# Causal attention in halves of 64 keys, in a fused attention and tanh-shrink kernel on one Trainium2 core

## The chip, the cores and the metric

The kernel runs on one core of one Trainium2 chip. The metric is the device time of one execution in microseconds (us), and lower is better. Engine names are those of the profile: PE is TensorE (its weight loads are a row of their own, PEld), DVE is VectorE, ACT is ScalarE, POOL is GpSimd and SP is SyncE. A letter q behind a name (SPq) means that engine's instruction queue.

## The reference

The first stage is causal linear attention with a decay `lam` per head; the second multiplies its output by `w_in`, takes `h - tanh(h)`, and multiplies by `w_out`.

```python
# q, k, v: (B=4, H=8, S=768, D=64) float32; lam: (8,)
Dmask = np.where(rel >= 0, lam[:, None, None] ** rel[None, :, :], 0.0)      # rel = i - j in a block
for b in range(nb):                                                        # blocks of 64 in the reference
    intra = np.einsum('bhic,bhjc->bhij', qb, kb) * Dmask[None]
    intra = np.einsum('bhij,bhjd->bhid', intra, vb)
    inter = np.einsum('bhid,bhde->bhie', qb * lam_pow[None], kv_state)
    out[:, :, sl] = intra + inter
    kb_dec = kb * rev_pow[None]                                            # lam ** (block - 1 - pos)
    kv_state = lam_block * kv_state + np.einsum('bhsd,bhse->bhde', kb_dec, vb)
x = out.transpose(0, 2, 1, 3).reshape(B * S, H * D)                         # (3072, 512)
h = x @ w_in                                                               # w_in (512, 2048)
return (h - np.tanh(h)) @ w_out                                            # w_out (2048, 512)
```

## The kernel before, in words

The kernel uses blocks of `BLK` = 128 positions, which gives the same result as the reference's 64. There are six groups `g` of one block each; a group holds that block of all four batches `b`, so 512 tokens. The eight heads are four pairs `p` of two heads `j` (head 2p + j). While the matrix products of group g run, the attention of group g + 1 is done in between. `attention(g)` makes two lists of pieces, one for the half (b = 0, 1) and one for (2, 3), and the code around the products places them: `att_transpose` (q and k with the head dimension on partitions), `att_scores`, `att_out`, `att_state`.

The two products are not plain: each is done by a scheme with seven smaller products instead of eight (`up`, `down`), for some of them twice in a row (`down_twice`, `inner_steps`). Their matmuls are full tiles of 128x128 weights against 128 or 256 moving columns. They fill nearly all of TensorE's time. The pieces of `w_out` sums come from DRAM into a ring of seven buffers `wb`, loaded by POOL (lines 602 to 608).

In this kernel every fp32 matmul of the program is two instructions in the trace, each with its weight load; I call each of the two a pass. The attention has four kinds of passes, named here as "contracted rows x weight columns, moving columns":

- `att_scores`, line 352: 64x128, 128 columns. The two heads j of a pair stand on partition halves, so two passes run side by side. One batch has 16 passes. The result `sp` (keys on partitions, queries on columns) is multiplied by the decay mask into `ss` on VectorE (line 356), 512 columns for each j.
- `att_out`, line 400: `state` against `qd`, 64x64, 128 columns, in the four quarters of the array. 32 passes for a half of two batches.
- `att_out`, line 406: `v` against `ss`, 128x64, 128 columns, 32 passes for a half. With line 400 it accumulates in `op`, which ScalarE copies to `xt` (line 410).
- `att_state`, line 374: decayed `k` against `v`, 128x64, 64 columns, 32 passes for a half. The decay of k is line 361 on VectorE.

In groups 0 and 1 q and k are transposed by TensorE (line 336); from group 2 on they are loaded in 32x32 blocks (line 143) and transposed by VectorE (line 331). k and v in natural order are loaded by one DMA of 256 KB each from SP's queue (line 131). Instructions marked with `keep_in_program_order` (or `tied`) keep their written order; the others are placed by a scheduler, engine by engine. Banks of TensorE's result memory for the attention come from one tag, `att`, with four buffers. The blocks of `w_in` and `w_out` are loaded (lines 205 to 210) and rounded by ScalarE and VectorE (lines 289 to 296) during the first 130 us; this is `weights(n)`.

Of the kernel before, what the change touches and what calls it, by code (L numbers as in the profile page):

```python
# [9 lines left out]
F32 = mybir.dt.float32  # L10
# [6 lines left out]
AL = mybir.AluOpType  # L17

BLK = 128
GB = 2  # L20
# [4 lines left out]
def kernel(  # L25
# [32 lines left out]
    nc = tc.nc  # L58
    B, H, S, D = q.shape
    NTOK, DM = out.shape  # L60
    DFF = moe_w_in.shape[1]
    NP = H // 2
# [10 lines left out]
    const = ctx.enter_context(tc.tile_pool(name="const", bufs=1))  # L73
    wpool = ctx.enter_context(tc.tile_pool(name="wpool", bufs=1))
    io = ctx.enter_context(tc.tile_pool(name="io", bufs=4))
    work = ctx.enter_context(tc.tile_pool(name="work", bufs=2))
# [13 lines left out]
    ident = const.tile([128, 128], F32)  # L90
    make_identity(nc, ident)
    lam_all = const.tile([128, H], F32)
    nc.scalar.dma_start(out=lam_all, in_=bass.AP(tensor=lam.tensor, offset=lam.offset, ap=[[0, 128], [1, H]]))

    mask = const.tile([128, 2, NP, BLK], F32)
    for j in range(2):
        for p in range(NP):
            h = 2 * p + j
            nc.vector.tensor_tensor_scan(out=mask[:, j, p, :], data0=lam_all[:, h:h + 1].to_broadcast([128, BLK]),
                                         data1=ident, initial=0.0, op0=AL.mult, op1=AL.add)  # L100

    fwd = const.tile([128, NP, BLK], F32)

# [8 lines left out]
            m *= 2  # L112


    bwd = mask.rearrange("s j p i -> s p j i")[:, :, :, BLK - 1:BLK].to_broadcast([128, NP, 2, D])

    lam_blk = fwd[:, :, BLK - 1:BLK][:, None, :, :].to_broadcast([128, 2, NP, D])

    def tied(yes, op):
        return tc.keep_in_program_order(op) if yes else op  # L120


    raw, late = {}, {}
# [3 lines left out]
    def load_natural(g, b, names):  # L127
        for name, src, bufs in (("q", q, 2), ("k", k, 3), ("v", v, 4)):
            if name in names:
                x = (qpool if name == "q" else io).tile([128, H, D], F32, name=f"{name}_nat", tag=name, bufs=bufs)  # L130
                op = nc.sync.dma_start(out=x, in_=src[b, :, ts(g, BLK), :].rearrange("h s d -> s h d"))  # L131
                tc.keep_in_program_order(op)
                raw[g, b][name] = x

    def load_blocks(g, b, names):
# [162 lines left out]
    def bank(name, tag, bufs):  # L298
        return psum.tile([128, 512], F32, name=name, tag=tag, bufs=bufs)
# [18 lines left out]
    state = const.tile([128, B, NP, D], F32)  # L318


    tr, sc, kdec, xt = {}, {}, {}, {}

    def att_transpose(g, bs):
        for b in bs:
# [17 lines left out]
                nc.vector.tensor_tensor(qd, qt, fwd, op=AL.mult)  # L342
            tr[g, b] = (qt, kt, qd)

    def att_scores(g, bs):
        for b in bs:
            qt, kt, _ = tr[g, b]

            sp = [bank("sp", "att", 4).rearrange("s (p i) -> s p i", p=NP) for _ in range(2)]
            for p in range(NP):  # L350
                for j in range(2):
                    tied(g == 0, nc.tensor.matmul(out=sp[j][:, p, :], lhsT=kt[ts(j, 64), p, :],  # L352
                                                  rhs=qt[ts(j, 64), p, :], start=True, stop=True))
            ss = work.tile([128, 2, NP, BLK], F32, name="ss", tag="ss")
            for j in range(2):
                tied(g == 0, nc.vector.tensor_tensor(ss[:, j], sp[j], mask[:, j], op=AL.mult))  # L356
            sc[g, b] = ss

    def att_decay(g, b):
        kp = raw[g, b]["k"].rearrange("s (p j) d -> s p j d", j=2)  # L360
        tied(g != 1, nc.vector.tensor_tensor(kp, kp, bwd, op=AL.mult))

    def att_state(g, bs):
        if g == NG - 1:
# [19 lines left out]
    def att_out(g, bs):  # L384
        half = bs[0] // 2
        xt[g, half] = xpool.tile([128, KI, HB], F32, name=f"xt{half}", tag=f"xt{half}")

        ops = [bank("op", "att", 4).rearrange("d (p b s) -> d p b s", p=2, b=2) for _ in range(2)]

        def dst(n, p, j):  # L390
            return ops[p // 2][ts(j if p < 2 else 1 - j, 64), p % 2, n, :]


        if g > 0:
            for n, b in enumerate(bs):
                for p in (0, 1):
                    for j in range(2):
                        r = ts(j, 64)
                        for pp in (p, p + 2):
                            nc.tensor.matmul(out=dst(n, pp, j), lhsT=state[r, b, pp, :], rhs=tr[g, b][2][r, pp, :],  # L400
                                             start=n == 0 and p == 0, stop=False, skip_group_check=True)
        for n, b in enumerate(bs):
            ss, vn = sc.pop((g, b)), raw[g, b]["v"]
            for p in range(NP):
                for j in range(2):
                    tied(g == 0, nc.tensor.matmul(out=dst(n, p, j), lhsT=vn[:, 2 * p + j, :], rhs=ss[:, j, p, :],  # L406
                                                  start=g == 0 and n == 0 and p % 2 == 0,
                                                  stop=n == 1 and p % 2 == 1, skip_group_check=True))
        for x in range(2):
            tied(g == 0, nc.scalar.activation(  # L410
                xt[g, half][:, 2 * x:2 * x + 2, :].rearrange("d p (b s) -> d p b s", b=2), ops[x], AF.Copy))
# [9 lines left out]
        xt[g] = dict(B11=b11, B21=b21, B22=b22, T1=tt[:, 0], T2=tt[:, 1], T3=b12, T4=tt[:, 2])  # L421

    def attention(g):
        pieces = [[(fn, g, bs) for fn in (att_transpose, att_scores, att_out, att_state)] for bs in ((0, 1), (2, 3))]
        pieces[1].append((att_sums, g, None))
        return pieces

# [133 lines left out]
    def twice(g, n):  # L561
        return n in TWICE and not (g == NG - 1 and n == 3)
# [154 lines left out]
            store(g, 12, o)  # L717
        yield

    def every(steps):  # L720
        for _ in steps:
            pass

    def down_end(g):

# [81 lines left out]
    def run(pieces):  # L807
        for fn, *args in pieces:
            fn(*args)


    for b in (0, 1):
# [4 lines left out]
    half = up_plain(0, (11, 21))  # L817
# [26 lines left out]
    p0, p1 = attention(1)  # L844
    load(B + 2)
    turns = [(1, 11, 1, ()), (1, 21, 1, ()), (1, 12, 1, ()), (1, 22, 1, ()), (2, 11, 2, p0[0:1]), (2, 21, 2, p0[1:2]),
             (3, 11, 1, ()), (3, 21, 1, p0[2:4]), (2, 12, 1, ()), (2, 22, 1, p1[0:1]), (3, 12, 1, p1[1:2]),
             (3, 22, 1, ())]
    for u, c, n, more in turns:
        every(up_plain(u, (c,)))  # L850
        weights(ready["done"] + n)
        run(more)
        if c == 22:
            sums_first(u)
            if u == 1:
                load_weights(NU * KI)
                load(2 * B)
                powers()
            if u == 2:
                sums_in(0)  # L860
    sums_out(0)
    run(p1[2:4])
    sums_out(1)
    weights(NU * KI + 6)
    load_weights(ready["done"] + WAHEAD)
    run(p1[4:])
    sums_late(0)
    for kt in range(KH):
        down_first(kt, (1, 2, 5, 4, 7, 6, 3) if kt + 1 < KH else (1, 2, 6, 5, 7, 3, 4))
# [17 lines left out]
    for g in range(1, NG):  # L887
        last = g == NG - 1
        p0, p1 = attention(g + 1) if not last else ([], [])
# [14 lines left out]
                run(p0[u - 2:u - 1])  # L904
        if twice(g, 4):
            sums_twice(g, 4)
        every(down(g, 2))
        run(p0[2:])
        sums_twice(g, 5)
        every(down_twice(g, 4, "z") if twice(g, 4) else down(g, 4))  # L910
        run(p1[0:1])
        sums_once(g, 21, 21, 11)
        sums_twice(g, 6)
# [1 line left out]
        run(p1[1:2])  # L915
        if twice(g, 7):
            sums_twice(g, 7)
        every(down_twice(g, 6, "z"))
        if twice(g, 3):
            sums_twice(g, 3)  # L920
        run(p1[2:])
        every(down_twice(g, 7, "w") if twice(g, 7) else down(g, 7))
        if last:
            down_end(g)
# [45 lines left out]
```

## Time and profile before

| | |
|---|---|
| time, three runs | 667.26, 668.35, 668.37 us; median 668.35 us |
| profiled execution | span 665.0 us from the first to the last instruction; its own total time is not on the page |
| what lies around the span | 668.35 - 665.0 = 3.3 us, by the median of the runs |
| PE busy | 653.9 us, 98% of the span |
| DVE busy | 480.1 us, 72% |
| ACT, POOL busy | 32%, 29% |
| granted TensorE clock | 1.000 |
| DMA | mean 183 GB/s |

A row of a group of instructions reads: line, engine, operation, out<-in by the program's names, shapes, count, then total busy time, mean ns of one, and the idle time before them with what ended it. Passes overlap on TensorE, so the mean of one (some 270 ns) is a latency; what a pass costs is the step from one start to the next.

### The profile page before, as it was taken

How to read it: one execution, taken by the hardware profiler on the slowest of the kernel's cores; microseconds unless marked ns; L12 is line 12 of the kernel's file. 1: busy time of each engine (PE TensorE's matmuls, PEld its weight loads, DVE VectorE, ACT ScalarE, POOL GpSimd, SP SyncE). 2: the span in 40 equal slices, each digit the busy share in tenths (PEclk: the TensorE clock that was granted, in tenths of full speed). 3: DMA queues.
4: the chain of work that ended last, by engine and by line, in shares of the span. 5: the costliest groups of instructions: out<-in, count | busy, mean ns of one | idle time of the engine just before them, and what ended most of it. 6: DMA issues, size and time to landing. Idle time of an engine off the chain costs nothing.

```text
span 665.0 us, 13269 instructions
## 1 busy us (share of the span) xinstructions
PE 653.9 (98%) x4992; PEld 594.7 (89%) x4992; DVE 480.1 (72%) x869; ACT 214.7 (32%) x413; POOL 195.8 (29%) x340
## 2 busy tenths in 40 slices
PE   8999999999999999999999999999999999999998
PEld 7788888888888999888999988999988899988897
DVE  4568898997778983579885379987368877357753
ACT  4778923423321112341112342112243112233110
POOL 0001416783112444001435101254301264400250
PEclk9999999999999999999999999999999999999999
DMA  9999936997345979425889543698731687610491
GB/s 216 231 205 263 300 123 215 352 316 219 81 93 145 303 221 276 80 35 135 226 247 277 146 74 73 165 286 255 216 72 38 186 260 258 222 37 1 116 295 64
DMA packets 158958, 121.74 MB, mean 183 GB/s; under 512 B 133872, under 2 KB 135024, under 8 KB 158896
## 3 DMA queue, kind: packets, MB, share of 16 engines
q0 software_dynamic: 26400, 86.27, 40.4%
q1 hardware_dynamic: 132352, 34.64, 25.3%
q8 instruction: 39, 0.64, 0.4%
q14 instruction: 23, 0.19, 0.1%
q10 hardware_dynamic: 144, 0.00, 0.0%
HBM read 100.67 MB, written 20.19 MB: 182 GB/s over the span
## 4 chain that ended last, share of the span: by engine, by line
PE 66%; issue 14%; DMA 8%; SPq 4%; POOL 3%; DVE 3%; ACT 1%; POOLq 0%; DVEq 0%; ACTq 0%
PE y L458 13%; PE y L693 12%; PE zw L693 9%; PE z L458 8%; PE y L542 4%; PE w L640 4%; PE y L640 4%; PE sp L352 2%; PE z L542 2%; DMA raw<-in_moe_w_in_dram 2%; PE h L748 2%; DMA wb<-fine 2%; PE op L406 2%; SPq L131 2%; SPq L143 1%
## 5 line engine op out<-in xcount | busy, mean ns | idle before, releaser
L605 POOL DMA_DIRECT2D wb<-fine x168 | 90.5, 539 | 170.3 <-PE y L693 55.9
L466 ACT ACTIVATE th<-g 128x512 f32<-128x512 f32 x76 | 47.6, 630 | 99.5 <-DVE g L471 34.2
L696 ACT ACTIVATE q<-y 128x128 f32<-128x128 f32 x96 | 26.6, 277 | 149.6 <-PE y L693 148.6
L458 PE MATMUL y<-xt,w 128*128 128x256 f32 x320 | 73.5, 380 | 0.0
L458 PEld LDWEIGHTS y<-xt,w 128*128 128x128 f32 x320 | 59.9, 190 | 8.5 <-ACT g L546 0.9
L467 DVE TENSOR_TENSOR g<-g,th 128x512 f32<-128x512 f32 x76 | 52.1, 689 | 21.1 <-ACT th L466 21.0
L693 PE MATMUL y<-wb,g 128*128 128x128 f32 x456 | 60.6, 278 | 0.0
L748 PE MATMUL h<-xt,w 128*128 128x256 f32 x256 | 58.0, 383 | 2.0 <-DVE w L296 2.0
L748 PEld LDWEIGHTS h<-xt,w 128*128 128x128 f32 x256 | 47.7, 190 | 9.9 <-DVE w L296 2.7
L693 PEld LDWEIGHTS y<-wb,g 128*128 128x128 f32 x456 | 55.1, 192 | 1.3 <-issue 0.3
L608 POOL DMA_DIRECT2D wb<-factors x44 | 23.8, 541 | 96.0 <-PE y L640 64.6
L693 PE MATMUL zw<-wb,g 128*128 128x128 f32 x304 | 40.3, 275 | 0.1
L458 PE MATMUL z<-tt,ws 128*128 128x256 f32 x160 | 38.1, 381 | 0.0
L458 PE MATMUL y<-tt,ws 128*128 128x256 f32 x160 | 37.8, 379 | 0.0
L458 PE MATMUL z<-xt,ws 128*128 128x256 f32 x160 | 37.8, 379 | 0.0
L693 PEld LDWEIGHTS zw<-wb,g 128*128 128x128 f32 x304 | 37.0, 192 | 0.2 <-DVE g L698 0.2
L640 PE MATMUL w<-wb,g 128*128 128x256 f32 x160 | 35.8, 382 | 0.0
L640 PE MATMUL y<-wb,g 128*128 128x256 f32 x160 | 35.3, 379 | 0.0
L356 DVE TENSOR_TENSOR ss<-sp,mask 128x512 f32<-128x512 f32 x48 | 31.1, 684 | 5.8 <-PE sp L352 5.8
L640 PEld LDWEIGHTS y<-wb,g 128*128 128x128 f32 x160 | 30.4, 190 | 4.1
L458 PEld LDWEIGHTS z<-xt,ws 128*128 128x128 f32 x160 | 30.4, 190 | 4.1
L640 PEld LDWEIGHTS w<-wb,g 128*128 128x128 f32 x160 | 30.1, 190 | 4.4
(178 smaller groups left out, 1292.6 us busy)
## 6 DMA issues: line engine op xcount, KB each, us to landing
wb<-fine POOLq DMA_DIRECT2D x168, 256.0 KB, 4.2
wb<-factors POOLq DMA_DIRECT2D x44, 256.0 KB, 4.5
v_nat<-in_v_dram SPq DMA_DIRECT2D x24, 256.0 KB, 5.2
wb<-fine_in POOLq DMA_DIRECT2D x24, 256.0 KB, 4.3
k_nat<-in_k_dram SPq DMA_DIRECT2D x20, 256.0 KB, 5.0
raw<-in_moe_w_out_dram POOLq DMA_DIRECT2D x10, 512.0 KB, 4.9
raw<-in_moe_w_in_dram SPq DMA_DIRECT2D x8, 512.0 KB, 6.0
raw<-in_moe_w_in_dram SPq DMA_DIRECT2D x16, 256.0 KB, 5.6
```

The costliest lines, as they stand in the source:

```text
L131: op = nc.sync.dma_start(out=x, in_=src[b, :, ts(g, BLK), :].rearrange("h s d -> s h d"))
L356: tied(g == 0, nc.vector.tensor_tensor(ss[:, j], sp[j], mask[:, j], op=AL.mult))
L458: nc.tensor.matmul(out=t[:, m, :], lhsT=wt[:, kt, ts(m, 128)], rhs=x[:, kt, :], start=first and m == 0 and kt == 0, stop=kt == 1, skip_gro ...
L466: nc.scalar.activation(th, src, AF.Tanh)
L467: nc.vector.tensor_tensor(dst(c), src, th, op=AL.subtract)
L542: nc.tensor.matmul(out=dst[:, ts(u, 128)], lhsT=a, rhs=b, start=x in (1, 2, 5) and u == 0, stop=True, skip_group_check=True)
L605: nc.gpsimd.dma_start(out=t.rearrange("p m c -> p (m c)"), in_=fine[TWICE.index(n_), SUB.index(x_)].rearrange("p u c -> p (u c)"))
L608: nc.gpsimd.dma_start(out=t, in_=factors[XAT[FACT[n_][1]]][:, 2 * x_:2 * x_ + 2, :])
L640: nc.tensor.matmul(out=t[:, m, :], lhsT=a[:, u, kt, ts(m, 128)], rhs=wb[:, kt, :], start=first and u == 0 and m == 0 and kt == 0, stop=u = ...
L693: nc.tensor.matmul(out=dst, lhsT=a[:, u, :], rhs=wb[:, ts(u, 128)], start=x in (1, 2) and u == 0, stop=u == NU - 1, skip_group_check=True)
L696: nc.scalar.activation(keep, dst, AF.Copy)
L748: tied(u == 0, nc.tensor.matmul(out=hm[c][:, m, :], lhsT=w1[u][:, i, a, ts(m, 128)], rhs=xt[0, t][:, i, :], start=m == 0 and i == 0, stop= ...
```

## The change

Each block of 128 keys is split in two halves of 64 (`HF`). An early key can meet all 128 queries; a late key can only meet the 64 late queries. So the scores of a head become one product of 64 early keys with 128 queries and one of 64 late keys with 64 queries. The quarter "late keys, early queries" of the masked matrix, which is zero, is no longer computed.

For heads 4 to 7 the two key halves are exchanged on the partitions: k and v of these heads are loaded with late keys on partitions 0 to 63 and early keys on 64 to 127. Therefore early scores of heads 0 to 3 fall on the lower partition half and those of heads 4 to 7 on the upper one, and four consecutive passes use the four quarters of the array. In `sp` and `ss` a head pair has three column groups of 64 (`c`): 0 is early keys with early queries, 1 and 2 hold early and late keys with late queries, which together fill all 128 partitions.

`att_out`'s line 406 becomes two: late queries take all 128 keys (128x64, 64 columns), early queries take 64 keys (64x64, 64 columns). The mask is built for this layout; its multiplication is 384 columns for each j instead of 512. The decay of k becomes two instructions of 256 columns, because the mask columns that it uses differ between the head halves. k and v loads become three DMAs each. The matmuls with `state` move out of `att_out` into a new step `att_read`, which runs right behind the scores of the half's first batch; the scores of the second batch, `att_out` and `att_state` are placed later, inside the products around them.

```diff
+    HF = BLK // 2
+    mask = const.tile([128, 4, 3, HF], F32)
...
+    for n in range(4):
+        for dst, x in ((mask[:, n, 0:2].rearrange("s c i -> s (c i)"), 0), (cross[:, n], 1)):
+            w = dst.shape[-1]
+            nc.vector.tensor_tensor_scan(out=dst, data0=lam_x[:, x, n:n + 1].to_broadcast([128, w]), data1=inj[:, 0:w],
+                                         initial=0.0, op0=AL.mult, op1=AL.add)
+    for a, to, src in ((1, 2, mask[:, :, 1]), (1, 1, cross), (0, 2, cross)):
+        nc.vector.tensor_copy(mask[ts(a, HF), :, to], src[ts(a, HF)])
...
-                op = nc.sync.dma_start(out=x, in_=src[b, :, ts(g, BLK), :].rearrange("h s d -> s h d"))
-                tc.keep_in_program_order(op)
+                if name == "q":
+                    tc.keep_in_program_order(
+                        nc.sync.dma_start(out=x, in_=src[b, :, ts(g, BLK), :].rearrange("h s d -> s h d")))
+                else:
+                    for rows, hs, at_ in ((slice(0, BLK), 0, 0), (slice(0, HF), NP, HF), (slice(HF, BLK), NP, 0)):
+                        n = rows.stop - rows.start
+                        part = src[b, hs:hs + NP, g * BLK + at_:g * BLK + at_ + n, :]
+                        tc.keep_in_program_order(nc.sync.dma_start(out=x[rows, hs:hs + NP], in_=part.rearrange("h s d -> s h d")))
...
+    def att_read(g, bs):
+        ops = [bank("op", "att", 4).rearrange("d (p b s) -> d p b s", p=2, b=2) for _ in range(2)]
...
+                            tc.keep_in_program_order(nc.tensor.matmul(
+                                out=dst(n, pp, j), lhsT=state[r, b, pp, :], rhs=tr[g, b][2][r, pp, :],
+                                start=n == 0 and p == 0, stop=False, skip_group_check=True))
...
-            for p in range(NP):
-                for j in range(2):
-                    tied(g == 0, nc.tensor.matmul(out=sp[j][:, p, :], lhsT=kt[ts(j, 64), p, :],
-                                                  rhs=qt[ts(j, 64), p, :], start=True, stop=True))
+            for q in range(2):
+                for j in range(2):
+                    for p in (q, q + 2):
+                        tied(g == 0 or (b % 2 == 1 and (q, j, p) == (0, 0, 0)), nc.tensor.matmul(out=sp[j][half(p, False), q, 0:2 + p // 2:1 + p // 2, :],
+                                                      lhsT=keys(p, j, False), rhs=qt[ts(j, 64), p, :], start=True, stop=True))
+            for q in range(2):
+                for j in range(2):
+                    for p in (q, q + 2):
+                        tied(g == 0, nc.tensor.matmul(out=sp[j][half(p, True), q, 1 + p // 2, :], lhsT=keys(p, j, True),
+                                                      rhs=qt[ts(j, 64), p, HF:BLK], start=True, stop=True))
...
+    def att_scores_read(g, bs):
+        att_scores(g, bs[:1])
+        att_read(g, bs)
...
-        kp = raw[g, b]["k"].rearrange("s (p j) d -> s p j d", j=2)
-        tied(g != 1, nc.vector.tensor_tensor(kp, kp, bwd, op=AL.mult))
+        for e in range(2):
+            kp = raw[g, b]["k"][:, ts(e, NP)]
+            tied(g != 1, nc.vector.tensor_tensor(kp, kp, bwd[e], op=AL.mult))
...
+                    tied(whole, nc.tensor.matmul(out=dst(n, p, j)[:, HF:BLK], lhsT=vn[:, 2 * p + j, :],
+                                                  rhs=ss[:, j, p % 2, 1 + p // 2, :],
+                                                  start=g == 0 and n == 0 and p % 2 == 0,
+                                                  stop=True, skip_group_check=True))
...
-                    tied(g == 0, nc.tensor.matmul(out=dst(n, p, j), lhsT=vn[:, 2 * p + j, :], rhs=ss[:, j, p, :],
-                                                  start=g == 0 and n == 0 and p % 2 == 0,
-                                                  stop=n == 1 and p % 2 == 1, skip_group_check=True))
+            for q in range(2):
+                for p in (q, q + 2):
+                    for j in range(2):
+                        r = ts(p // 2, HF)
+                        tied(whole, nc.tensor.matmul(out=dst(n, p, j)[:, 0:HF], lhsT=vn[r, 2 * p + j, :],
+                                                      rhs=ss[r, j, q, 0, :], start=False, stop=True,
+                                                      skip_group_check=True))
...
-        pieces = [[(fn, g, bs) for fn in (att_transpose, att_scores, att_out, att_state)] for bs in ((0, 1), (2, 3))]
+        pieces = [[(att_transpose, g, bs), (att_scores_read, g, bs), (att_scores, g, bs[1:]), (att_out, g, bs),
+                   (att_state, g, bs)] for bs in ((0, 1), (2, 3))]
...
-        every(down(g, 2))
-        run(p0[2:])
+        product = down(g, 2)
+        steps(product, 2)
+        run(p0[2:3])
+        every(product)
         sums_twice(g, 5)
-        every(down_twice(g, 4, "z") if twice(g, 4) else down(g, 4))
+        product = down_twice(g, 4, "z") if twice(g, 4) else down(g, 4)
+        steps(product, 2)
+        run(p0[3:])
+        every(product)
...
-        every(down_twice(g, 6, "z"))
+        product = down_twice(g, 6, "z")
+        steps(product, 3)
+        run(p1[2:3])
+        every(product)
```

## The prediction

> **What bounds the kernel now.** I read the page's busy times first, then the chain that ended last in order of time, then TensorE's groups by shape, then TensorE's rows in a short window, and SP's queue at the start.
>
> ```profile
> span 665.0 us, 13269 instructions
> PE 653.9 (98%) x4992; PEld 594.7 (89%) x4992; DVE 480.1 (72%) x869; ACT 214.7 (32%) x413; POOL 195.8 (29%) x340
> ```
>
> TensorE is busy 98% of the span at a granted clock of 1.000; by windows it is busy 25.3 of the first 30 us, and from there to the end of the chain nearly all of every window (30.0 of 30 us from 80 to 110, 50.0 of 50 from 170 to 220). So a microsecond of TensorE work taken out is a microsecond of time, unless a wait takes its place. The time of the runs' median is 668.35 us, 3.3 us above the span; I take those 3.3 us as unchanged. The attention's share, from TensorE's groups by shape (the last two numbers ahead of the idle time are busy us and mean ns):
>
> ```profile
> L352 PE MATMUL sp<-qt,kt 64*128 64x128 f32 x384 | 25.2, 279 | 1.4 <-ACT kt L338 1.4
> L406 PE MATMUL op<-ss,v_nat 128*64 128x128 f32 x384 | 23.6, 275 | 0.0
> L374 PE MATMUL kv<-v_nat,k_nat 128*64 128x64 f32 x320 | 11.3, 223 | 0.0
> L400 PE MATMUL op<-qd,state 64*64 64x128 f32 x320 | 11.0, 275 | 0.0
> ```
>
> Only 71 of 665 us are attention, and the change touches the first two rows, 48.8 us. Next the timeline of TensorE, second half of one group; the first column is the start, and what a block costs is the distance to the next start:
>
> ```profile
> 229.76 2.06 PE L352 MATMUL sp<-qt,kt 64*128 64x128 f32 x32
> 231.75 1.16 PE L693 MATMUL y<-wb,g 128*128 128x128 f32 x8
> 232.74 1.06 PE L693 MATMUL zw<-wb,g 128*128 128x128 f32 x8
> ...
> 238.20 1.10 PE L400 MATMUL op<-qd,state 64*64 64x128 f32 x32
> 239.23 1.97 PE L406 MATMUL op<-ss,v_nat 128*64 128x128 f32 x32
> 241.03 1.10 PE L374 MATMUL kv<-v_nat,k_nat 128*64 128x64 f32 x32
> 242.06 0.71 PE L693 MATMUL y<-wb,g 128*128 128x128 f32 x4
> ```
>
> Blocks cost 1.99, 1.03, 1.80 and 1.03 us. Inside a block the starts step evenly; per pass, once running: line 352 56.0 ns (pairs 112 apart), line 400 27.3 ns (four starts within 20 ns, next four 109 ns after the first), line 406 54.5 ns, line 374 29.0 ns (pairs 58 apart), full tiles 112 ns for 128 columns. The rest is change of tile shape: the last pass before and the first pass after take 90 to 100 ns and 50 to 100 ns longer than their step. The two changes around line 352 cost 0.39 us in all, the three around the other block 0.51.
>
> **The change on TensorE, for one half of a group (two batches).** Before: 32 passes x 56.0 + 32 x 54.5 + 32 x 27.3 (state) + 32 x 29.0 (kv) + 0.90 for five changes of shape = 6.23 us. It repeats in ten halves (groups 1 to 5).
>
> After, by the order of instructions on TensorE:
> - First block: scores of batch one (16 early passes, 64x64 with 128 columns; 16 late, 64x64 with 64 columns) and 32 state passes, all one shape. Early passes have line 400's shape: 16 x 27.3 = 0.44; state 0.87; in and out 0.15 + 0.19.
> - Second block: scores of batch two, 0.44 early, 16 late; in and out 0.34.
> - Third block: 32 passes 128x64 with 64 columns for late queries, line 374's shape: 32 x 29.0 = 0.93; 32 passes 64x64 with 64 columns for early queries; kv 0.93; four changes, 0.14 to 0.19 each, 0.62.
>
> Sum: 2 x 0.44 + 0.87 + 0.93 + 0.93 + 1.29 = 4.90 us, and 64 passes of a shape that no row has: 64x64 with 64 columns, at x ns. The half gains 1.34 us - 64x. It breaks even at x = 21 ns.
>
> Bounds for x: from above line 400, the same quarters with twice the columns, 27.3 ns; from below line 374, whose 64 columns need 58 ns for a pair: if four quarters run in those 58 ns, x = 14.5. Line 400 shows four different quarters starting within 20 ns, so four fit into 58. A pass and its weight load are two instructions, so this needs one each 7.3 ns; in three places TensorE's queue, released from a semaphore wait, reaches the next semaphore 16 instructions later 143 ns after, at most 8.9 ns each, and it runs some 34 instructions ahead of the array, which covers such short bursts. I take 14.5: both rows it is built from scale with columns (109 ns for 128, 58 for 64). Then a half gains 1.34 - 0.93 = 0.41 us. In the last group no kv follows, one change less: 0.56. Sum: 8 x 0.41 + 2 x 0.56 = **4.4 us gained**. In group 0 TensorE waits for data; its saving counts nothing.
>
> A rule speaks against it. The Trainium skill, "TensorE: Matmul & The Clock Gate", section "Wait — 56ns, not 53.3ns?", says that the step between matmul starts never falls under about 25 ns however few columns. Line 400's starts 5 to 8 ns apart contradict it between quarters; if it held as a mean, the sum would be a loss (first rival).
>
> **What is added elsewhere.**
> - VectorE: 48 mask products shrink from 512 to 384 columns. 512 take 684 ns, 256 take 420 (line 703): about 552, so 48 x 0.13 = 6.3 us less. The decay of k: 20 x (2 x 420 - 686) = 3.1 us more. VectorE is 72% busy and not on the path: net nothing. What matters is its order. In a group's first half the decays now stand behind line 698's work, which waits for the second product of the following step, and kv comes 1.8 us after that product; the decays (0.7 + 4 x 0.35 us) end about when they are needed. The second batch's mask product has 2 to 3 us before its use. In group 1 it stands behind a `th` that ScalarE ran late at 70.7 us. I charge 0.4 us.
> - Mask at the start: four scans of 128, four of 64 and some small copies instead of eight of 128, about 1 us more on VectorE after `lam` lands at 3.85 us. The first decay ran at 7.19 us: hidden, or 0.4 us.
> - Loads: 44 loads of k and v become 132 DMAs. SP's queue at the start:
>
> ```profile
> 0.74 0.44 SPq L131 DMA_DIRECT2D q_nat<-in_q_dram  x1
> 1.25 0.57 SPq L131 DMA_DIRECT2D k_nat<-in_k_dram  x1
> 1.86 1.78 SPq L131 DMA_DIRECT2D v_nat<-in_v_dram  x1
> 3.69 0.93 SPq L131 DMA_DIRECT2D q_nat<-in_q_dram  x1
> ...
> 18.84 2.45 SPq L210 DMA_DIRECT2D raw<-in_moe_w_in_dram  x1
> ```
>
>  An issue takes 0.38 to 0.57 us when nothing holds it and 1.1 us here, where the transfers are the limit (DMA share 0.89, 1.12, 1.07 in the first three windows of 10 us). The `w_in` block whose landing at 27.2 us lets TensorE run from 30 us stands behind eight loads of k and v. Upper bound: 16 issues x 0.43 = 6.9 us; lower bound nothing, as bytes and their 256-byte rows are the same. The near row is the saturated share: 0.4 us. Only eight DMAs can be out at once (each issue waits on its lane's semaphore), now of smaller size; the loads of group 1 stand ahead of `w_in` blocks that TensorE waited 0.9 us for at 66 us: 0.3 us. Later loads have tens of us.
> - POOL's ring: TensorE waited 1.5 us near 218 and 0.9 us near 327 us for `wb` pieces. Shorter attention blocks give the ring less pause. Of 4.4 us I let 0.4 come back as such waits; at most the whole 4.4.
>
> Sum: -4.4 + 0.4 + 0.4 + 0.3 + 0.4 = -2.9 us: span 662.1, time **665.4 us**.
>
> **Rivals.**
> 1. *The small quarters do not run at 14.5 ns* (slower). If a pass of 64 columns costs as much as one of 128, or the queue feeds no faster, x = 25 to 27.3, a half loses 0.26 to 0.41 us, ten halves 2.3 to 3.8 us; with 1.5 us of costs 672.2 to 673.7 us. It decides from x = 21 (with those costs 19). For it: no row has this shape, and instructions double. Against: line 374's step. By the skill's 25 ns: 672.2. Chance 0.13.
> 2. *The loads push the weights back* (slower). If issues do not hide behind transfers, TensorE starts up to 6.9 us later: -4.4 + 6.9 + 1.1 = +3.6, 672.0 us. It decides from 3.3 us of delay. Against: the share of 1.1. Chance 0.07.
> 3. *Waits take the gain back* (no change). VectorE's decays and mask products come late by 0.3 us in ten halves, or the `wb` ring sets the pace: 668 us. Chance 0.15.
> 4. The passes do not do what the diff says: the order shows 64x64 passes in four quarters in turn, as line 400. Chance under 0.01.
>
> **How the numbers follow.** The forecast holds 0.65; its own range is 663.4 (4.4 gained, little lost, fewer `wb` waits) to 667.2. A measurement of this kernel can tell about 0.2%, 1.3 us: faster means under 667.0. The forecast gives 0.63 of that and a little to same; rival 3 gives most of same and some on both sides; rivals 1 and 2 are slower, 0.20. Range for 8 in 10: 663.4 to 670.0, which leaves out most of rivals 1 and 2.
>
> **What would show it.** Right: 64-column passes of line 466 of the changed kernel step four in about 58 ns, the third block costs 2.9 us and the first 1.9, and the distance between the same products in groups 2 to 5 shrinks by 0.8 us per group. Wrong: a step near 100 ns for four; TensorE's row of w_in products starting later than 31 us; idle TensorE ahead of kv released by VectorE.

## The result and the profile after

The changed kernel takes 671.99 us, the median of five runs (671.46 to 673.23), against 668.35 us for the kernel before on the same chip: ratio 1.0059, 95% interval 1.0041 to 1.0078. It is slower, by 2.7 to 5.2 us; the forecast was 2.9 us faster. In a later set of runs (c_after below) the ratio was 1.0108 (1.0084 to 1.0133).

The profiled execution of the changed kernel took 671.77 us at a span of 669.9 us. The page:

```profile
span 669.9 us, 14964 instructions
PE 652.6 (97%) x5760; PEld 590.8 (88%) x5760; DVE 475.9 (71%) x898; ACT 215.2 (32%) x413; POOL 196.6 (29%) x340
```

TensorE is busy 1.3 us less and the span is 4.9 us longer: the new time is 6.2 us of idle time. The busy time also holds stretches at a lower clock, shown below. The groups by shape, as before (busy us, mean ns, idle us ahead):

```profile
L399 PE MATMUL sp<-qt,kt 64*64 64x128 f32 x384 | 16.0, 282 | 1.4 <-ACT kt L357 1.4
L456 PE MATMUL op<-ss,v_nat 128*64 128x64 f32 x384 | 13.8, 225 | 0.0
L433 PE MATMUL kv<-v_nat,k_nat 128*64 128x64 f32 x320 | 12.8, 235 | 2.1 <-DVE k_nat L420 2.0
L404 PE MATMUL sp<-qt,kt 64*64 64x64 f32 x384 | 10.1, 221 | 0.0
L466 PE MATMUL op<-ss,v_nat 64*64 64x64 f32 x384 | 8.3, 224 | 0.0
```

Lines 399 and 404 take the place of line 352, 456 and 466 that of 406; 433 is kv, which now has 2.0 us of waiting for the decay (line 420). TensorE's timeline, second half of group 2, the same stretch as shown of before:

```profile
236.43 0.67 PE L399 MATMUL sp<-qt,kt 64*64 64x128 f32 x16
...
238.14 1.16 PE L754 MATMUL y<-wb,g 128*128 128x128 f32 x8
...
241.01 0.67 PE L399 MATMUL sp<-qt,kt 64*64 64x128 f32 x16
241.50 0.41 PE L404 MATMUL sp<-qt,kt 64*64 64x64 f32 x16
241.84 1.23 PE L754 MATMUL zw<-wb,s 128*128 128x128 f32 x8
...
245.78 1.15 PE L456 MATMUL op<-ss,v_nat 128*64 128x64 f32 x32
246.86 0.69 PE L466 MATMUL op<-ss,v_nat 64*64 64x64 f32 x32
247.49 1.15 PE L433 MATMUL kv<-v_nat,k_nat 128*64 128x64 f32 x32
248.57 1.16 PE L754 MATMUL y<-wb,g 128*128 128x128 f32 x8
```

The blocks take 1.71, 0.83 and 2.79 us from start to next start, 5.33 us against 5.85 us before. A row of eight product passes beside a block takes 0.98 to 1.09 us to the next start (between products mostly 0.89 or 0.90), and there are two more such places than before. So a half of groups 2 to 4 that waits for nothing takes 5.90 us against 6.24, borders included: 0.34 us less. In these blocks the passes of lines 404 and 466 step 14.5 ns each, four in 58 ns.

The loss lies early. SP's queue at the start:

```profile
1.24 1.99 SPq L151 DMA_DIRECT2D k_nat<-in_k_dram  x3
3.27 1.91 SPq L151 DMA_DIRECT2D v_nat<-in_v_dram  x3
...
23.87 1.26 SPq L229 DMA_DIRECT2D raw<-in_moe_w_in_dram  x2
```

Three issues take 1.9 to 2.2 us, where one took 0.4 to 1.8. The fourth `w_in` block is issued in two halves from 23.87 us on (before: 18.84). The second half lands at 28.93 us (27.18): 5 us later at the issue are 1.75 us at the landing. The first row of eight w_in products that has all of group 0's transposes ahead of it starts at 29.03 us (27.34). The next row waits for the rounded weights of that block, and it is 1.75 us late too (first before, then changed):

```profile
30.00 6.31 PE L748 MATMUL h<-xt,w 128*128 128x256 f32 x28 [0.67 <-DVE w L296]
31.75 4.58 PE L813 MATMUL h<-xt,w 128*128 128x256 f32 x20 [0.72 <-DVE w L315]
```

Then the chain that ended last, in group 1:

```profile
80.18 0.64 PE kv L433 x16
80.82 0.02 issue
80.84 0.37 SPq L151
...
81.26 0.61 SPq L151
...
81.92 7.67 DMA k_nat<-in_k_dram
...
89.73 0.41 PE tp L355 x2
```

`k` has three buffers. The load of k for the last block of group 1 waits until kv of the first half has read a buffer, then three issues and a landing follow; TensorE stands still for 3.12 us. Before, 32 passes of the products of group 0 (7.0 us) lay between this kv and the transposes. In the changed kernel the order on TensorE has product (2,12), 16 passes, ahead of the first half's transposes; 16 passes (3.5 us) are left as cover. Windows behind that wait (TensorE's clock is the third number from the end):

```profile
84.00:90.00 6.00, 2.88 (x22) 2.34 (x21) 4.48 (x9) 5.72 (x11) 4.68 (x7) 1.00 1.05 324
90.00:96.00 6.00, 6.00 (x54) 4.80 (x56) 4.19 (x9) 1.19 (x2) 0.89 (x2) 0.72 0.81 291
```

At a clock of 0.72, the 16 passes at 89.97 us take 5.24 us instead of 3.55. The start of the down products is 7.0 us late (104.38 against 97.40 us): most of it is the 1.75 us of the start, the 3.1 us of this wait and the 1.7 us of lower clock behind it. From there to the end the changed kernel wins back 2.1 us.

### The profile page after: what moved, and what is told of

It is laid out like the page before. It is cut to its first block, busy times and chain, and to the rows that moved or that the text cites. A ratio compares the mean times of both kernels' runs of the same rounds, so it can differ in the third digit from the quotient of the medians.

```text
span 669.9 us, 14964 instructions
## 1 busy us (share of the span) xinstructions
PE 652.6 (97%) x5760; PEld 590.8 (88%) x5760; DVE 475.9 (71%) x898; ACT 215.2 (32%) x413; POOL 196.6 (29%) x340
## 4 chain that ended last, share of the span: by engine, by line
PE 78%; issue 9%; DMA 6%; POOL 2%; SPq 2%; ACT 1%; DVE 1%; POOLq 0%; ACTq 0%
PE y L519 12%; PE y L754 11%; PE zw L754 8%; PE z L519 8%; PE h L813 7%; PE acc L843 7%; PE w L701 4%; PE y L603 4%; PE y L701 4%; PE z L603 2%; SPq L151 2%; DMA k_nat<-in_k_dram 2%; DMA wb<-fine 2%; PE sp L399 2%; PE op L456 1%
## 5 line engine op out<-in xcount | busy, mean ns | idle before, releaser
L813 PE MATMUL h<-xt,w 128*128 128x256 f32 x256 | 60.3, 391 | 3.7 <-DVE w L315 3.7
L813 PEld LDWEIGHTS h<-xt,w 128*128 128x128 f32 x256 | 48.7, 194 | 12.1 <-DVE w L315 3.2
L519 PEld LDWEIGHTS z<-tt,ws 128*128 128x128 f32 x160 | 29.4, 190 | 4.8 <-DVE g L555 0.8
```

Source lines behind the costliest of these rows:

```text
L519: nc.tensor.matmul(out=t[:, m, :], lhsT=wt[:, kt, ts(m, 128)], rhs=x[:, kt, :], start=first and m == 0 and kt == 0, stop=kt == 1, skip_gro ...
L813: tied(u == 0, nc.tensor.matmul(out=hm[c][:, m, :], lhsT=w1[u][:, i, a, ts(m, 128)], rhs=xt[0, t][:, i, :], start=m == 0 and i == 0, stop= ...
```

## The experiments

Ratios are against the kernel before on the same chip, with 95% intervals. The offsets in the table are of one profiled execution each, in us against the profile before (27.34, 97.40 and 665.0 us): the first steady row of w_in products (the one at 27.34 us above), the first down product, the span.

| kernel | w_in row | down product | span | ratio (interval) |
|---|---|---|---|---|
| changed | +1.7 | +7.0 | +4.9 | 1.0059 (1.0041 to 1.0078) |
| c_after, the same again | +1.7 | +8.6 | +8.7 | 1.0108 (1.0084 to 1.0133) |
| e1_before_split | +2.6 | +7.8 | +8.4 | 1.0101 (1.0080 to 1.0122) |
| e11_before_split0 | +2.3 | +5.2 | +4.3 | 1.0053 (1.0036 to 1.0069) |
| e4_before_short | +0.2 | +1.1 | +0.8 | 1.0026 (1.0011 to 1.0041) |
| e2_after_k4 | +1.3 | +12.1 | +11.6 | 1.0163 (1.0139 to 1.0188) |
| e3_after_order | +2.6 | +4.4 | +4.0 | 1.0083 (1.0064 to 1.0102) |
| e12_best | +1.9 | +3.9 | +4.3 | 1.0052 (1.0032 to 1.0071) |
| e5_after_decay | +1.9 | +9.7 | +9.6 | 1.0094 (1.0071 to 1.0118) |
| e13_hybrid | 0.0 | -0.1 | +6.0 | 1.0104 (1.0081 to 1.0127) |
| e14_hybrid_ring | +0.3 | +1.2 | +3.8 | 1.0059 (1.0037 to 1.0081) |
| e15_hybrid_ring_decay | +0.1 | -0.3 | +1.7 | 1.0028 (1.0014 to 1.0042) |
| e16_before_ring | +1.3 | +1.3 | +0.1 | 0.9995 (0.9979 to 1.0012) |
| e17_hybrid_late | -0.3 | -0.2 | +0.6 | 1.0014 (1.0000 to 1.0027) |
| e18_best | +0.7 | +0.1 | -4.6 | 0.9946 (0.9926 to 0.9965) |
| e19_after_ring_decay | +2.7 | +6.0 | +2.5 | 1.0061 (1.0036 to 1.0087) |

**c_after**: the changed kernel without an edit.

> The changed kernel once more, beside the other runs of this set, to compare them with on the same chip. Expected: 0.4 to 0.8% above the kernel before, as in its first runs (ratio 1.0059); the first steady row of w_in products at 28.5 to 30 us, the first down product 6 to 10 us later than before's 97.4 us.

Measured 675.12 us against 667.66. The late start and the wait for k (3.20 us at 88.1 us) came again; the loss is 7.2 us (5.6 to 8.9), more than in the first set, where it was 3.9. Between the two profiled executions lie 3.7 us: 1.6 up to the down products, and most of the rest is a lower clock behind the wait ahead of kv in group 2 (0.66 from 224 to 228 us), which the first profile does not have.

**e1_before_split**: the kernel before with split loads alone.

```diff
-                op = nc.sync.dma_start(out=x, in_=src[b, :, ts(g, BLK), :].rearrange("h s d -> s h d"))
-                tc.keep_in_program_order(op)
...
+                for rows, h0, h1 in parts:   # k, v: heads 0-3 whole; heads 4-7 rows 0-63; rows 64-127
+                    part = src[b, h0:h1, g * BLK + rows.start:g * BLK + rows.stop, :]
+                    tc.keep_in_program_order(nc.sync.dma_start(out=x[rows, h0:h1], in_=part.rearrange("h s d -> s h d")))
```

> The kernel before, with nothing changed but the loads of k and v, each in three DMAs of the same shapes as in the changed kernel (heads 0 to 3 whole, heads 4 to 7 in two halves of 64 rows), without the exchange. Theory (the loads cost at two places): the first steady row of w_in products starts 1.5 to 1.7 us later than before's 27.34 us, and in group 1 the load of k for block 3 lands 1.2 us later after its issue, so that the second half's transposes wait about 1 us for it; time 670 to 672 us. Rival A (the issues at the start are all of the loss): the start is later by as much, nothing waits for k in group 1, 670 us. Rival B (the loads are free, the loss is in the new attention blocks): within 0.5 us of 668.35.

6.7 us slower (5.3 to 8.1), more than every theory gave. The attention blocks are those of before, and yet the same 16 passes of product (2,12) stand early: the order follows from the split loads. TensorE's timeline shows the wait for k, here in two parts:

```profile
88.17 0.41 PE L340 MATMUL tp<-ident,k_nat 128*128 128x128 f32 x2 [0.60 <-DMA k_nat<-in_k_dram]
90.36 0.66 PE L340 MATMUL tp<-ident,k_nat 128*128 128x128 f32 x2 [1.78 <-DMA k_nat<-in_k_dram]
```

So the loads alone make a loss as large as that of the whole change, with the same late start and the same wait. Rival B falls.

**e11_before_split0**: as e1, but only where `g == 0`.

> The kernel before with only the eight loads of k and v of group 0 split into three DMAs each; all later loads whole. Theory (the loss by split loads, 6.8 us with all of them split, has two places, the start and group 1): the first steady row of w_in products 1.7 to 2.6 us later than 27.3 us, no wait for k in group 1, the first down product 2 to 4 us later than 97.4 us; 2 to 4 us above the kernel before. Rival A (all of it is the start): 6 to 7 us above. Rival B (the start's delay is made up for by w_in blocks that are in time anyway): within 1 us of the kernel before.

3.5 us slower (2.4 to 4.6): about half of e1's loss is the start, the other half group 1. Rivals A and B fall. The row that starts at 30.00 us before starts 3.5 us later here and 3.0 us later in e1. Seven of the eight matmuls of product (2,12) stand where they stood before, and no wait for k is over 0.4 us.

**e4_before_short**: the kernel before with only the order of group 1 changed.

```diff
-             (3, 11, 1, ()), (3, 21, 1, p0[2:4]), (2, 12, 1, ()), (2, 22, 1, p1[0:1]), ...
+             (3, 11, 1, ()), (3, 21, 1, ()), (2, 12, 1, p0[2:4]), (2, 22, 1, p1[0:1]), ...
```

> The kernel before, with whole loads, and only the order of group 1 changed as it came about in the changed kernel: the product (2,12) of group 0 ahead of the first half's kv, so that 16 instead of 32 passes (3.5 us) stand between kv and the second half's transposes. Theory (the short cover makes the wait): kv comes 3.5 us later, the k load of block 3 is issued at about 78.7 us and lands at 85 to 86 us; TensorE waits 2 to 3.5 us for it, and about 1 us more goes by a lower clock afterwards: 670.5 to 672.5 us on a chip where before is 667.4 to 668.4. Rival (a whole load lands sooner, and the wait in the changed kernel comes from the splitting): wait under 1 us, 668 to 669 us.

1.7 us slower (0.7 to 2.7). kv at 77.24, the load issued at 77.92 us; it lands 7.0 us later, and TensorE goes on then (the row names a VectorE instruction as releaser, but the four transposes read the k that landed at 84.9 us):

```profile
85.01 0.63 PE L336 MATMUL tp<-ident,k_nat 128*128 128x128 f32 x4 [1.69 <-DVE gS L765]
```

So the short cover makes 1.7 us of the 3.1 us of waiting in the changed kernel. The other 1.4 us go by difference to splitting: the third issue starts 1.08 us after the first and lands 7.7 us later, 1.75 us more in all than the 7.0 us here.

**e2_after_k4**: the changed kernel with `("k", k, 4)` for `("k", k, 3)`.

> The changed kernel with four buffers for k instead of three, so that the load of k for block 3 of group 1 need not wait for kv of the first half. Theory: the wait of 3.1 us ahead of the second half's transposes (at 86.6 to 89.7 us) goes, with it the granted clock of 0.72 from 90 to 96 us (1.6 us): 4.5 to 5 us less, of which up to 1.3 come back as waits for pieces of weights before 208 us; 667 to 668.5 us. Rival A (the DMA engines are full there, the load lands late whenever it is issued, or what it pushes back lands late): a wait of 2 us or more stays at the same place or in the w_out products, 670 to 672 us. Rival B (the wait costs nothing, because TensorE would have waited for weights instead): 672 us.

Slower, 678.63 us: the theory is refuted as far as time goes. The load is issued at 73.3 us and the wait for it is gone, but TensorE now waits 0.3 us for ScalarE, then 1.3 and 2.1 us for VectorE's `g` and `ss` (92.4 and 101.0 us), and the clock is 0.79 and 0.78 in the two windows from 100 to 108 us. So the wait for k hid later VectorE work, and taking it away brought that out. Besides, TensorE waited 3.2 us for rounded weights at 30.6 us in this execution (0.7 in the changed kernel's first profile, 1.7 in its second), which the extra buffer does not explain; that stays open.

**e3_after_order**: the changed kernel with products (2,12), (2,22) and the first half's kv tied in the written order.

> The changed kernel with the products (2,12) and (2,22) of group 0 kept behind the first half's kv in group 1, as they stood in the kernel before: 32 passes (7.0 us) instead of 16 (3.5 us) between kv and the second half's transposes. Theory: kv comes earlier, by 3.5 us less what the products of w_in's last quarter wait for their rounding in the meantime (1.8 us at 69 to 74 us now), so the load is issued 1.5 to 3.5 us earlier, the wait for k is under 1 us, the clock stays at 1.0: 668 to 670 us. Rival A (the wait only moves: the products of the last quarter wait for rounding by the whole 3.5 us more): 671.5 to 672 us, with waits for DVE w ahead of kv in place of the one for k.

The order on TensorE is as before, the wait for k in group 1 is gone, and the down product is 4.4 us late instead of 7.0 or 8.6. Waits for rounded weights grew from 3.7 to 5.8 us: part of the wait moved. At 672.82 us, 5.5 us above the kernel before, the theory's time is refuted, and by time e3 can't be told from the changed kernel (1.0083 lies between its two ratios).

**e12_best**: the changed kernel with e3's ties, v of two blocks of group 0 and of all of group 1 issued from POOL.

```diff
+                        eng = nc.gpsimd if (name == "v" and (g, b) < (2, 0) and (g, b) not in ((0, 2), (0, 3))) else nc.sync
...
+        for b in {(2, 11): (0, 1), (3, 11): (2, 3)}.get((u, c), ()):
+            load_natural(1, b, "v")
```

> The changed kernel with the loads taken out of SP's way: v of the first two blocks of group 0 issued from POOL's queue, v of all blocks of group 1 from POOL's queue behind its first w_out loads, and the products (2,12) and (2,22) kept behind the first half's kv. Theory (the new attention blocks gain, SP's issues and the short cover lose): first steady row of w_in products within 0.7 us of 27.3, no wait over 1 us for k in group 1, first down product at 97 to 100 us; the gain of groups 2 to 5 (about 3 us) stays; 2 to 4 us below the kernel before, 664 to 666 us. Rival A (v comes late from POOL's queue: kv at 12 us or op at 78 us waits for v_nat): 667 to 670 us. Rival B (the transfers, not the issues, set the pace at the start): the steady row still at 28.5 us or later, 668 to 671 us.

3.5 us slower than before (2.1 to 4.7). The start stays 1.9 us late although SP has six issues fewer: kv of the first two blocks came 2.3 us later than before, as k and v arrived together and the clock was 0.69 from 10 to 20 us, and the load of k behind it waited for its buffer. The DMA share of the first three windows of 10 us was 0.90, 0.96 and 0.93, against 0.73, 0.97 and 0.96 in the changed kernel and 0.89, 1.12 and 1.07 before. Moving issues to another queue did not cure the start (rival B fits). The Trainium skill, "SBUF — State Buffer", section "Can I just issue two DMAs to hit both halves?", says that two transfers, each on half of the partitions, run one after the other instead of together; that speaks against loads of 64 rows. No run here separates it from the number of issues.

**e5_after_decay**: the changed kernel, decays earlier in the first half of groups 2 to 4.

```diff
             sc[g, b] = ss
+            if 1 < g < NG - 1 and b == 1:
+                att_decay(g, 0)
+                att_decay(g, 1)
...
-            if g > 0:
+            if g == 1 or (g > 1 and b > 1):
                 att_decay(g, b)
```

> The changed kernel with the decays of k for the first half of groups 2 to 4 called right behind the second batch's mask product instead of behind the work of the next product on VectorE. Theory: TensorE's wait of 2.0 us ahead of kv in group 2 (at 223 us) goes; 0.5 to 1 us of it returns as waits for pieces of w_out at 226 us: 670.5 to 671.5 us. Rival A (the ring of pieces gives the pace in group 2, so all of it returns): 672 us. Rival B (the decays now delay the sums that the next products read): a new wait of 1 us or more for s, 672 to 673 us.

In the changed kernel VectorE comes to the four decays at 223.05 us, behind work of the next products, and kv waits:

```profile
223.61 0.58 PE L433 MATMUL kv<-v_nat,k_nat 128*64 128x64 f32 x12 [2.04 <-DVE k_nat L420]
```

In e5 this wait is gone, and waits in all three groups take its place (waits of TensorE from 110 us on):

```profile
PE y L757 <- DMA wb<-fine: 1.8, 3, 0.8
PE zw L757 <- DVE gS L762: 1.1, 1, 1.1
PE zw L757 <- DMA wb<-fine: 1.1, 2, 0.8
```

Gaps from 200 us on add up to 4.6 us, against 2.8 in the changed kernel, and the time does not differ from the changed kernel's (1.0094 lies between its two ratios). This fits rival A: the ring of pieces sets the pace once the blocks are shorter. e14 and e15 test it.

**e13_hybrid**: groups 0 and 1 with the old functions, whole loads and old mask; from group 2 on the changed ones.

```diff
+                if name == "q" or g < GB:      # whole loads for groups 0 and 1
...
+        if g < GB:
+            return att_scores_old(g, bs)       # likewise att_out, att_decay, attention
...
+            if g == 1 and u == 2:
+                quarters()                     # builds the mask of the quarters
```

> Groups 0 and 1 as in the kernel before (whole loads, whole scores, its own mask), the quarter blocks and the split loads from group 2 on; the masks of the quarters are built behind group 1. Theory (the loss of the changed kernel lies in groups 0 and 1; from group 2 on the blocks gain 0.33 us per half and 0.5 in the last group's, 3.0 us, and the late decays in group 2 cost 2 us, with up to 1.5 us of lower clock behind that wait): no difference up to 100 us, then 3 us gained and 2 to 4 lost: within 1 us of the kernel before. Rival A (the blocks gain their 3 us and nothing takes it back): 2.5 to 3 us below. Rival B (split loads cost from group 2 on as well): more than 1.5 us above, with waits for k or v or blocks of q and k.

No difference up to the down products, then 6 us lost at a place made by the edit. VectorE came to the mask at 144 us and waited there 5.05 us for a scratch buffer that a store of `fine` sums still read. The weight sums of the next products stood behind it, and TensorE stood still for 3.00 us up to 158.21 us. After that wait the clock was 0.81 and 0.77 in two windows of 4 us, another 1.7 us. So the time of e13, e14 and e15 says nothing on the question; their traces from group 2 on do, below.

**e14_hybrid_ring, e15_hybrid_ring_decay, e16_before_ring**: nine buffers for `wb` (e14), with e5's decays (e15), and eight buffers in the kernel before, where nine do not fit (e16).

```diff
-            t = late["pool" if r == "wb" else r].tile([128, 2, 256], F32, name="wb", tag=r, bufs=RING)
+            t = late["pool" if r == "wb" else r].tile([128, 2, 256], F32, name="wb", tag=r, bufs=RING + 2 if r == "wb" else RING)
```

> The same with nine buffers instead of seven in the ring of w_out pieces (wb). Theory: the waits of TensorE for wb pieces (0.8 to 2.6 us in all from group 2 on with the quarter blocks) go, the wait for the decays in group 2 stays: 0.7 to 2 us below e13_hybrid. Rival (the pieces are late because of the transfers, not because of their buffers): as e13_hybrid within 0.5 us.

> The same with nine buffers, and the decays of k for the first half of groups 2 to 4 called right behind the second batch's mask product. Theory: neither the decays nor the pieces are waited for, the gain of the blocks is left whole: 2.5 to 4 us below the kernel before, 663.5 to 665 us where before is 667.5. Rival (with the decays' wait gone the pieces come late in all three groups, as where the decays alone were moved, 4.6 us of gaps): 0 to 1 us below the kernel before.

> The kernel before with eight buffers instead of seven in the ring of w_out pieces (one more is all that fits), to see what the ring alone gives. Theory: its two waits for wb pieces (0.7 us each) go: 0.7 to 1.4 us below the kernel before. Rival: no difference.

Time from the first scores of group 2 to the last instruction, in the traces: before 462.5 us, e13 462.5, e14 460.9, e15 458.5, e16 461.2. The blocks alone change nothing (their 3 us go to kv's wait and the pieces), nine buffers give 1.7 us with them, eight give 1.3 us without, and the early decays give 2.4 us on top. By time, e14 is 2.3 us and e15 4.2 us below e13, but both stay above the kernel before, e15 at 669.03 us where its theory had 663.5 to 665. e16's whole time is not different from before: its theory (0.7 to 1.4 us less) is not borne out. What nine buffers would give without the blocks is not tested.

**e17_hybrid_late, e18_best, e19_after_ring_decay**: e13 and e15 with the mask built one or two instructions at a time between products at 166 to 179 us; and the changed kernel with e15's ring and decays.

```diff
+                if g == 1 and u > 0:
+                    next(built, None)          # built = quarters(), now a generator
```

> As e13_hybrid (groups 0 and 1 as before, quarter blocks and split loads from group 2 on), with the masks of the quarters built piece by piece between 160 and 185 us, where VectorE has room. Theory: the gap of 3.0 us at 155 us and the lower clock behind it go; no difference from the kernel before up to 200 us (within 0.7 us), from there to the end no difference either (3 us gained by the blocks, 2.1 us lost ahead of kv in group 2, 0.5 to 1 us more waits for pieces): within 1 us of the kernel before. Rival (the quarter blocks or the split loads lose from group 2 on): 2 us or more above.

> The same with nine buffers in the ring of w_out pieces and the decays of the first half of groups 2 to 4 early. Theory: as in e15_hybrid_ring_decay 4.0 us are gained from the first scores of group 2 to the end, and nothing is lost before: 3.3 to 4.5 us below the kernel before, ratio 0.993 to 0.995; faster than both kernels. Rival (the masks still come in the way of VectorE's sums): 1 us below or less, with a gap before 200 us.

> The changed kernel with nine buffers in the ring and the early decays, its groups 0 and 1 untouched. Theory: 5.7 to 7.5 us are lost up to the first scores of group 2, 4 us are gained from there: 1.5 to 3.5 us above the kernel before, ratio 1.002 to 1.005. Rival (the loss of groups 0 and 1 is made up for by waits that go elsewhere): within 0.5 us of the kernel before or below it.

e17: 0.9 us slower (0.0 to 1.8): from group 2 on the change as written gives nothing. Its trace takes 464.3 us from the first scores of group 2 on, 1.7 us more than e13's, the price of a lower clock behind the wait ahead of kv. e18: **663.36 us, 3.6 us below the kernel before (2.3 to 4.9)**, the fastest of all. Its page, and all its waits of TensorE from 110 us on:

```profile
span 660.4 us, 14396 instructions
PE 650.3 (98%) x5504; PEld 590.2 (89%) x5504; DVE 478.8 (73%) x898; ACT 214.6 (33%) x413; POOL 195.9 (30%) x340
```

```profile
PE zw L828 <- DVE gS L833: 0.7, 1, 0.7
PE acc L917 <- DVE s L926: 0.3, 1, 0.3
```

From the first scores of group 2 on e18 takes 458.2 us, 4.4 less than before: 3.0 of it are the blocks, 1.0 is less idle time of TensorE (1.6 us before, 0.7 in e18).

e19 is 4.1 us slower than before (2.4 to 5.8), at the upper end of what was expected (1.5 to 3.5) or above it: in the profiled execution 3.5 us are won behind the first down product, and the loss of groups 0 and 1 stays.

## Why the prediction was wrong, point by point

The step that failed is the price of the split loads: 0.4 us at the start and 0.3 us in group 1, where the runs show 6.7 us for them alone (e1). Term by term:

- **The blocks** (0.41 us per half, x = 14.5): the mechanism was right and x exact; as a mean over different quarters, the step between passes contradicts the floor of the first rival. The first sign that the prediction named for being right, four passes in about 58 ns, is there. The half gains 0.34 us: it takes 5.90 us where the prediction has 5.83, because its eight changes of shape cost 1.37 us and not 1.29. Ten halves give some 3.7 us, 3.0 of them from group 2 on (six at 0.34, two at 0.5). In e18 they are time.
- **Loads at the start** (0.4 us): 3.5 us by e11. The prediction took the rate at which SP issued whole loads, held by the transfers, for that of split ones; but three issues take 1.9 us where one took 1.1, and DMA's share in the first 10 us fell from 0.89 to 0.73. So the DMA engines had idle time that whole loads did not leave them. Whether the number of issues or the size of the loads makes the delay stays open, as e12 took six issues off SP and cured nothing. The prediction's upper bound (6.9 us) held the truth.
- **Loads of group 1** (0.3 us): about 3.3 us, e1 less e11, which are of two sets and each known to 1.1 to 1.4 us. The prediction looked at the w_in blocks behind these loads; it did not look at the load that waits for its own buffer, nor at what covers it. The changed order alone costs 1.7 us of this in the kernel before (e4).
- **VectorE's order** (0.4 us): the decays were expected "about when they are needed"; in groups 3 and 4 they were, in group 2 kv waited 2.0 us. Mask products measured 550 ns (552 reckoned), four decays 1.43 us (1.4): sizes right, place wrong.
- **The ring** (0.4 us, at most the whole gain): direction right. Behind late decays it cost no more than before (0.7 us of waits for pieces against 1.4); without that wait it took the gain (2.9 us in e5).
- **The clock** was no term. In the changed kernel's profile it fell at 12 to 16 us and at 88 to 96 us (1.7 us each, by windows of 4 us); in the profile before it stayed at 1.00 to the end of the span.
- **What lies around the span** (3.3 us): 1.9 us where time and span are known of the same execution of the changed kernel (671.77 less 669.9). For the kernel before it is mostly 1.9 us in the later sets, at times 2.5 to 3.4. The prediction took the median time of three runs and the span of another execution, so its 3.3 us are no measurement.

The sum by the runs: start 3.5, group 1 3.3, groups 2 to 5 0.9 (e17), 7.7 us together, against 7.2 us (5.6 to 8.9) for the changed kernel in a later set. This takes it that the losses add up, which is not shown: in the changed kernel's own two profiles the row of 30.00 us is 1.8 and 2.7 us late and group 1 adds 5.2 and 5.9 us, so that more of the loss falls into group 1 than in e1. In the first set the whole loss was 3.9 us (2.7 to 5.2); why its first profile has 1.6 us less loss up to the down products is open.

Rival 2 (loads push the weights back, 672.0 us) came nearest, and both signs that the prediction named against itself are there: the w_in row later than 31 us, and kv released by VectorE. That its 672.0 us meet the measured 671.99 is luck: it puts 6.9 us at the start, where no profile is more than 3.9 us late by that row, and takes the gain of the blocks as time.

## What to carry to other kernels

When a load is split, follow it to its buffer: what frees it, which instructions lie between that and its reader, and whether the new order leaves them there. A gain on the busiest engine is time only while its suppliers keep up; here the shorter blocks paid only with whole loads in the first two groups, two more buffers in the ring and an earlier decay (e18). An idle stretch of TensorE of 2 to 3 us can cost another 1.7 us in the clock behind it.

## What the runs showed of the hardware

- **The clock behind idle time.** Behind each idle stretch of 3.0 to 3.2 us in the middle of a kernel the granted clock fell to 0.50 to 0.81 in windows of 4 us (the changed kernel, c_after, e13, e14, e15), and 1.7 us were lost (3.4 in e15). A window laid on the fall shows 0.50 throughout (from 90.3 to 93.6 us in the changed kernel, from 156.0 to 162.7 in e15). After 1.9 to 2.9 us in group 2 it fell to 0.58 to 0.67 for one window in e2, e3, e12, e17 and c_after, and not at all in the changed kernel's first profile (2.04 us), e13 (2.13 us) and e14 (2.93 us). In group 1 it fell behind 1.4 us in e5 (up to 98.7 us) and not behind 1.5 us in e12 (up to 94.4 us). The Trainium skill, "TensorE: Matmul & The Clock Gate", section "What's actually happening", puts it down to an activity window of about 3.4 us that runs freely and halves the clock. The loss of 1.7 us agrees with half the clock for one such window; these runs show that an idle stretch well under 2 us can be enough and one of 2.9 us need not be.
- **Four quarters in turn**: 64x64 passes with 64 columns step 14.5 ns as a mean (four in 58 ns), half of the 29.0 ns of 128x64.
- **Issues on SP**: in the first 15 us of the changed kernel each part of a split load took SP 0.6 to 0.7 us, with 64 rows or with 128, so a load in three parts takes 1.9 to 2.0 us. Whole loads took 0.4 to 0.6 us where nothing held them.
- **Spread**: with split loads the first transposes of group 1 came 1.6 to 5.3 us later than before in nine profiles (the 3.9 us of 18 passes that stand ahead in some of them taken out); with whole loads -0.8 to +1.2 us in seven.
